# Second SiLU matmul of a three-part kernel: weight sums stationary instead of moving, groups of 1,024 tokens, weight sums streamed

## Chip, cores and metric

One core of a Trainium2 chip runs the whole program. The metric is the time of one execution on the device in microseconds (us); less is better. The number to forecast is the median time of the changed kernel.

## What is computed

Attention with pooled keys gives `x` (4,608 tokens, 512 wide), then two feed-forward blocks follow. The change lies in the second block's last matmul.

```python
x = attn_out.transpose(0, 2, 1, 3).reshape(B * S, H * D)   # 4608 x 512, pooled attention
h = x @ w_in; e = exp(h - max(h)); solu = h * e / sum(e)     # first block, 1024 wide
x = layernorm(solu) * g_ln @ w_out                           # 4608 x 512
h = x @ w2_in                                                # second block, 2048 wide
g = h / (1 + exp(-h))                                        # SiLU
out = g @ w2_out                                             # 4608 x 512, float32
```

## The kernel before

All matmuls are in 32-bit form with each operand split into a high part and a low part (`hi` by a copy on ACT, `lo` by a subtraction on DVE), so that one product of two blocks is three matmuls: high by high, high by low, low by high.

Three parts follow each other. The first, to about 600 us, is attention and the first block. The second multiplies by `w2_in` and applies SiLU: 12 passes (`n`) of four windows (`i`), each window seven products (`product`, L750; tile `m`). It leaves `g`, transposed (features on partitions), in DRAM tiles `gd`, six tiles of 768 tokens. The third part, "the last stage" in what follows, multiplies `g` by `w2_out` (L967, tile `op`). This is the part that changes.

Both SiLU matmuls use Winograd's form of Strassen's scheme: of a 2 x 2 block product seven products are made in place of eight, of sums of blocks. In the last stage the seven sums of `w2_out` are made ahead, during passes 3 to 10 (`w2o_block`, L860), split and written to DRAM as `wod`. The seven sums of `g` are made on the spot.

The products are named after the operand made of `g`: A11, A12 and A22 are raw blocks, S1A, S2A, S3A and S4A sums. The last stage walks over 9 groups of 512 tokens (`c`), 4 sets of contracted features (`s`) and 7 products (`j`). In every one of the 252 steps (`n`, 12 matmuls each) the tokens are the stationary operand (128 x 128) and the weight sum the moving one, 256 columns. All 14.7 MB of weight sums are loaded once and stay in SBUF. `load_g` (L899) fetches the raw blocks of a set, `sums_g` (L919) makes two sums on POOL (tile `s`), `prepare` (L927) makes two more on DVE in place (tile `gr`) and splits the operand into a ring of nine tiles `gt2` (`NRING`), nine steps ahead of the matmul. `combine` (L975) adds a finished product from PSUM to the others on ACT, DVE and POOL and writes `out`. Every engine runs its list in order. The engines' lists in the second and last part are in the order in which the code is written, and every DMA of the last stage stands on SP's list (14 weight loads in pass 11 stand on ACT's).

The second part takes its slots from a table: `plan(n, [(at, f), ...])` puts `f` into slot `at` of 28 in pass `n`, between the products.

Of the kernel before, what the change touches and what calls it, by code (L numbers as in the profile page):

```python
# [40 lines left out]
GO = 512  # L41
NGO = NT // GO
# [7 lines left out]
NSET = FC2 // 4  # L50
NRING = 9
UNITS = ((0, 1, 2), (3,), (4, 5), (6, 7))
# [36 lines left out]
def pooled_attention__solu__silu_kernel(  # L89
# [83 lines left out]
    wod = [dram.tile([P, 7, len(u), 2, 256], F32, tag=f"wod{u[0]}", name="wod") for u in UNITS]  # L173
# [678 lines left out]
    wo, graw, ring = {}, {}, {}  # L852
# [41 lines left out]
    def load_part(u, j, w, eng, first=0, last=None):  # L894
        eng.dma_start(w[:, first:last].bitcast(F32), wod[u][:, j, first:last])
        for i, f in enumerate(UNITS[u]):
            wo[f, j] = w[:, i]

    def load_g(q):  # L899
        c, s = divmod(q, NSET)  # L900
        if q % 3 == 1:
            raw = [pools["wx"].tile([P, 2, GO], F32, tag=f"a{h}", name="gr") for h in range(2)]
        else:
            raw = pools["gr" if q % 3 else "x2r"].tile(
                [P, 2, 2, GO], F32, tag="gr" if q % 3 else "x2r", name="gr")
# [11 lines left out]
    sums = {}

    def sums_g(q, temps):  # L919
        raw = graw[q]  # L920
        a11, a21, a22 = raw[0][:, :, :256], raw[0][:, :, 256:], raw[1][:, :, 256:]
        s1, s2 = (temps(k).rearrange("p (f d) -> p f d", d=256) for k in (1, 2))
        nc.gpsimd.tensor_tensor(s1, a21, a22, op=ALU.add)  # L923
        sub(nc.gpsimd, s2, s1, a11)
        sums[q] = s1, s2

    def prepare(n):  # L927

        q, j = divmod(n, 7)
        raw = graw[q]  # L930
        a11, a21, a12, a22 = (raw[i][:, :, 256 * k : 256 * k + 256] for i in range(2) for k in range(2))
        s1, s2 = sums[q]
        if j == S3A:
            sub(nc.vector, a21, a11, a21)
        src = (a11, s2, s1, a21, a12, a12, a22)[j]
        r = n % NRING
        if r < 7:
            t = pools["wq0"].tile(
                [P, 2, 512], F32R, tag=f"w{(L11, L12, S2, S1, S3, L22, S4)[r]}", name="gt2"
            )  # L940
        else:
            t = pools["wr"].tile([P, 2, 512], F32R, tag=f"w2r{r - 7}", name="gt2")
        ring[n] = t.rearrange("p w (f t) -> p w f t", f=2)
        nc.scalar.activation(ring[n][:, 0], src, AF.Copy)  # L944

        def rest():
            sub(nc.vector, ring[n][:, 1], src, ring[n][:, 0].bitcast(F32))
            if j == A12:
                sub(nc.vector, a12, a12, s2)

        return rest

    o_t = {}

    def product2(n):
        q, j = divmod(n, 7)
        c, s = divmod(q, NSET)
        if s == 0:
            o_t[c, j] = bank("op")
        op = o_t[c, j]  # L960
        t = ring.pop(n)
        for i in range(2):
            w = wo[2 * s + i, j]
            for h in range(2):
                ts = slice(h * P, (h + 1) * P)
                for m, (l, r) in enumerate(((0, 0), (0, 1), (1, 0))):
                    nc.tensor.matmul(  # L967
                        op[:, 256 * h : 256 * h + 256], t[:, l, i, ts], w[:, r],
                        start=(s == i == h == m == 0),
                        stop=(s == NSET - 1 and i == h == 1 and m == 2),  # L970
                    )

    m_t = {}

    def combine(c, j):  # L975
        b = o_t.pop((c, j)).rearrange("p (h d) -> p h d", h=2)

        def temp(name):
            m_t[name] = pools["m2"].tile([P, 512], F32, tag=name, name=name).rearrange(
                "p (h d) -> p h d", h=2)  # L980
            return m_t[name]

        def add(eng, dst, x, y):
            eng.tensor_tensor(dst, x, y, op=ALU.add)

        if j == 0:
            m_t["o"] = pools["ob"].tile([P, 2, 2, DM], F32, tag="ob", name="ob")
            nc.scalar.activation(temp("m1"), b, AF.Copy)
            return
        c11, c12, c21, c22 = (  # L990
            m_t["o"][:, h, :, 256 * d : 256 * d + 256] for h in range(2) for d in range(2)
        )
        r0 = c * GO
        rows = [out[r0 + 256 * h : r0 + 256 * h + 256].rearrange("(t p) d -> p t d", p=P) for h in range(2)]
        if j == 1:
            add(nc.vector, temp("u2"), b, m_t["m1"])
        elif j == 2:
            nc.scalar.activation(temp("m5"), b, AF.Copy)
            add(nc.gpsimd, c12, m_t["u2"], m_t["m5"])
        elif j == 3:  # L1000
            add(nc.vector, temp("u3"), b, m_t["u2"])
            add(nc.gpsimd, c22, m_t["u3"], m_t["m5"])
        elif j == 4:
            add(nc.vector, c11, b, m_t["m1"])
        elif j == 5:
            add(nc.vector, c12, b, c12)
            nc.sync.dma_start(rows[0], m_t["o"][:, 0])
# [160 lines left out]
    banks[:] = [5]  # L1168
# [10 lines left out]
    for n in range(N2):  # L1179
# [28 lines left out]
        if n == N2 - 1:  # L1208
            early = lambda j: pools["te"].tile([P, 3, 2, 256], F32R, tag=f"t{j}", name="w2o")
            work = [(0, lambda: load_g(0)), (8, lambda: load_g(1))]  # L1210
            units = {}

            def two(j):
                units[j] = early(j)
                load_part(0, j, units[j], nc.scalar, 0, 2)

            for j in range(7):
                work += [(3 * j + 1, lambda j=j: two(j)),
                         (21 + j, lambda j=j: load_part(0, j, units[j], nc.scalar, 2))]
            s0 = lambda k: pools["wr"].tile([P, 512], F32, tag=f"w2r{k - 1}", name="s")  # L1220
# [16 lines left out]
    for name in ("gr", "ob", "m2", "w2o"):  # L1237
        open_pool(name, 1, "left")
    load_g(2)
    for j in range(7):  # L1240
        tag = ("raw", "raw", "raw", "w", "w", "w", "sign")[j]
        w = stage.tile([P, 1, 2, 256], F32R, tag=tag, name="w2o", bufs=1 if j == 6 else 3)
        load_part(1, j, w, nc.sync)
    load_g(3)

    def late_part(u):
        for j in range(7):
            w = pools["w2o"].tile([P, 2, 2, 256], F32R, tag=f"w{u}{j}", name="w2o")
            load_part(u, j, w, nc.sync)

    late_part(2)

    def s_tmp(k):
        return pools["m2"].tile([P, 512], F32, tag=f"s{k}", name="s")

    NM = 7 * NSET * NGO
    sums_g(1, s_tmp)
    prepare(7)()
    prepare(8)()
    for n in range(NM):  # L1260
        q, j = divmod(n, 7)
        c, s = divmod(q, NSET)
        product2(n)
        if s == NSET - 1:
            combine(c, j)
        m = n + NRING
        if m < NM:
            if m % 7 == 0 and m // 7 + 2 < NSET * NGO:
                load_g(m // 7 + 2)
                if m == 14:  # L1270
                    late_part(3)
            if m % 7 == 5 and m // 7 + 1 < NSET * NGO:
                sums_g(m // 7 + 1, s_tmp)
            prepare(m)()
# [40 lines left out]
```

## Time and profile before

| | |
|---|---|
| median of 3 runs | 1317.07 us (1317.04 to 1319.51) |
| profiled execution, own time | 1319.98 us |
| its span, first to last instruction | 1318.2 us |
| granted TensorE clock, mean | 0.996 of full speed |
| PE busy, share of the span | 1267.8 us, 96% |
| DVE, ACT, POOL busy | 933.3, 750.2, 507.4 us |
| last stage on PE | 949.17 to 1312.05 us, 3,024 matmuls |

PE is TensorE's matmuls, PEld its weight loads, which lie beside the matmuls. DVE is VectorE, ACT ScalarE, POOL GpSimd, SP the engine that issues DMAs (SPq in a row). A row of the chain that ended last gives when a piece starts, how long it lasts and how many instructions it has. A matmul's own "duration" is its latency, so the pace of a stream of matmuls is read from starts, or from a piece's length divided by its count.

### The profile page before, as it was taken

Reading aid. Unit: us, or ns where it says so; the run is one execution under the profiler, and the core shown is the slowest. Engines: PE = TensorE matmul, PEld = TensorE weight load, DVE = VectorE, ACT = ScalarE, POOL = GpSimd, SP = SyncE. Lnnn points to the kernel's source line nnn. Section 1 sums busy time; section 2 is a strip of 40 time slices with the busy share of each in tenths; the row PEclk is TensorE's granted clock in tenths of the full one; section 3 lists DMA queues with packets and bytes.
Section 4 is the critical chain, followed back from the end, with each engine's and each line's share of the span. In section 5 each row is a group of like instructions: output and inputs, shape, how many; then the busy total and the mean of one; then the engine's idle time right before and its main releaser. Section 6 shows DMA issues by size and latency. Waiting matters only on the chain.

```text
span 1318.2 us, 23218 instructions
## 1 busy us (share of the span) xinstructions
PE 1267.8 (96%) x8192; PEld 1191.3 (90%) x8192; DVE 933.3 (71%) x1426; ACT 750.2 (57%) x1915; POOL 507.4 (38%) x725
## 2 busy tenths in 40 slices
PE   3689999999999999999999999999999999999998
PEld 3578888888888888889999999999999999999998
DVE  6998567776867665665767776666477777778774
ACT  4786566565666565545767777676544444444442
POOL 5666344434443433432324333332134433324331
PEclk9999999999999999999999999999999999999999
DMA  7755345445423411033776697775995443354340
GB/s 223 236 156 178 94 145 151 141 148 154 146 83 105 140 61 73 24 128 118 287 287 253 242 352 271 253 261 205 347 390 171 131 129 121 104 161 129 128 129 33
DMA packets 110101, 226.98 MB, mean 172 GB/s; under 512 B 10784, under 2 KB 44576, under 8 KB 108448
## 3 DMA queue, kind: packets, MB, share of 16 engines
q1 hardware_dynamic: 107968, 219.98, 49.9%
q10 hardware_dynamic: 2016, 5.51, 1.2%
q8 instruction: 65, 1.06, 0.3%
q14 instruction: 52, 0.43, 0.1%
HBM read 141.56 MB, written 83.89 MB: 171 GB/s over the span
## 4 chain that ended last, share of the span: by engine, by line
PE 81%; DVE 5%; ACT 5%; POOL 4%; DMA 2%; issue 2%; SPq 0%; POOLq 0%; ACTq 0%; DVEq 0%
PE op L967 28%; PE m L750 25%; PE hp L448 10%; PE xp L512 8%; PE xp L513 4%; ACT pr L335 2%; PE sp L317 2%; PE tp L497 2%; PE av L422 1%; DMA raw<-vm 1%; PE pm L371 1%; DVE w L148 1%; DMA wr<-w2of 1%; POOL e L483 1%; DVE w L151 1%
## 5 line engine op out<-in xcount | busy, mean ns | idle before, releaser
L967 PE MATMUL op<-w2o,gt 128*128 128x256 f32 x3024 | 363.0, 284 | 0.0
L967 PEld LDWEIGHTS op<-w2o,gt 128*128 128x128 f32 x3024 | 363.0, 192 | 0.0
L750 PE MATMUL m<-t,w2s 128*128 128x384 f32 x2016 | 351.5, 335 | 2.2 <-ACT u L832 1.1
L750 PEld LDWEIGHTS m<-t,w2s 128*128 128x128 f32 x2016 | 349.1, 188 | 4.4 <-ACT u L832 1.8
L512 PE MATMUL xp<-ln,w1oh 128*128 128x512 f32 x576 | 208.9, 404 | 2.0 <-DVE ln L130 1.9
L533 DVE TENSOR_TENSOR gt<-gr,gt 128x512 fp32r<-128x512 f32 x180 | 161.2, 925 | 59.3 <-ACT gt L944 59.0
L944 ACT ACTIVATE gt<-gr 128x512 fp32r<-128x512 f32 x180 | 106.1, 625 | 143.8 <-DVE gr L533 133.0
L513 PE MATMUL xp<-ln,w1ol 128*128 128x256 f32 x576 | 162.4, 282 | 0.0
L335 ACT ACTIVATE pr<-sp,st 128x72 f32<-128x72 f32 x288 | 88.4, 331 | 86.2 <-POOL st L327 86.1
L512 PEld LDWEIGHTS xp<-ln,w1oh 128*128 128x128 f32 x576 | 109.0, 189 | 25.5 <-DVE ln L130 2.5
L448 PE MATMUL hp<-w1ih,xTh 128*128 128x512 f32 x288 | 116.8, 406 | 1.9 <-DVE e L467 1.7
L448 PE MATMUL hp<-w1il,xTh 128*128 128x512 f32 x288 | 113.3, 394 | 1.3 <-POOL w1il L162 1.3
L448 PE MATMUL hp<-w1ih,xTl 128*128 128x512 f32 x288 | 113.6, 394 | 0.9 <-DMA raw<-vm 0.9
L513 PEld LDWEIGHTS xp<-ln,w1ol 128*128 128x128 f32 x576 | 110.1, 191 | 0.1
L923 POOL TENSOR_TENSOR s<-gr 128x512 f32<-128x512 f32 x36 | 58.0, 1611 | 126.9 <-DVE gt L533 72.7
L533 POOL TENSOR_TENSOR tt<-x2r 128x768 f32<-128x768 f32 x22 | 43.4, 1971 | 81.6 <-DMA x2r<-x2d 44.2
L944 ACT ACTIVATE gt<-s 128x512 fp32r<-128x512 f32 x72 | 43.4, 625 | 51.6 <-POOL s L533 31.6
L533 POOL TENSOR_TENSOR s<-s,gr 128x512 f32<-128x512 f32 x36 | 50.0, 1389 | 48.1 <-DVE gr L533 31.0
L448 PEld LDWEIGHTS hp<-w1ih,xTh 128*128 128x128 f32 x288 | 54.6, 190 | 13.7 <-DVE e L467 2.3
L129 ACT ACTIVATE ln<-tp 128x512 fp32r<-128x512 f32 x72 | 39.3, 596 | 48.2 <-PE tp L497 47.8
L448 PEld LDWEIGHTS hp<-w1ih,xTl 128*128 128x128 f32 x288 | 54.5, 189 | 13.2 <-DVE xTl L130 1.5
L448 PEld LDWEIGHTS hp<-w1il,xTh 128*128 128x128 f32 x288 | 54.7, 190 | 11.3 <-POOL w1il L162 1.6
(137 smaller groups left out, 2160.6 us busy)
## 6 DMA issues: line engine op xcount, KB each, us to landing
gr<-gd SPq DMA_DIRECT2D x48, 512.0 KB, 4.8
x2r<-x2d SPq DMA_DIRECT2D x12, 1536.0 KB, 7.5
gd<-ga SPq DMA_DIRECT2D x96, 192.0 KB, 3.1
gd<-gb SPq DMA_DIRECT2D x48, 384.0 KB, 3.2
wod<-wo SPq DMA_DIRECT2D x56, 256.0 KB, 2.5
gr<-gd SPq DMA_DIRECT2D x48, 256.0 KB, 4.2
q<-qT SPq DMA_DIRECT2D x36, 256.0 KB, 3.7
raw<-kT SPq DMA_DIRECT2D x32, 288.0 KB, 3.8
```

The costliest lines, as they stand in the source:

```text
L129: nc.scalar.activation(hi, src, AF.Copy)
L317: nc.tensor.matmul(sp[done : done + n, p // 2, (p % 2) * 2 * SP : (p % 2 + 1) * 2 * SP], q[:, p, done : done + n], kbd[b % 2][:, p, :], st ...
L335: nc.scalar.activation(pr[:, g, h], sv[:, g, h], AF.Exp, scale=SCALE, bias=st[:, 0, g, h : h + 1], accum_out=st[:, 1, g, h : h + 1],)
L448: nc.tensor.matmul(hp[:, f], l, r, start=(n == 1 and m == 0), stop=(n == KC and m == 2))
L497: nc.tensor.transpose(tp[:, k * P : (k + 1) * P], e[:, f, k * P : (k + 1) * P], ident)
L512: nc.tensor.matmul(xp, w1oh[:, k, cs], ln[:, k], start=(k == 0), stop=False)
L513: nc.tensor.matmul(xp[:, :GW], w1ol[:, k, cs], ln[:, k, 0], start=False, stop=(k == FC1 - 1))
L533: eng.tensor_tensor(dst, a, b, op=ALU.subtract)
L750: nc.tensor.matmul(to, wt[:, a, o : o + P], tk[:, b, k], start=(start and k == 0 and m == 0), stop=(k == 1 and m == 2), skip_group_check=n ...
L923: nc.gpsimd.tensor_tensor(s1, a21, a22, op=ALU.add)
L944: nc.scalar.activation(ring[n][:, 0], src, AF.Copy)
L967: nc.tensor.matmul(op[:, 256 * h : 256 * h + 256], t[:, l, i, ts], w[:, r], start=(s == i == h == m == 0), stop=(s == NSET - 1 and i == h ...
```

## The change

The last stage is written anew. What it computes is the same.

- The weight sum is now the stationary operand (two blocks of 128 output features, `blocks`) and the tokens are the moving one, 512 columns (256 in the last group). `out` comes out transposed, 512 x 4,608, and the host turns it round.
- There are 5 groups: four of 2 x 512 tokens and one of 2 x 256. A group is 56 steps: each of the seven products runs over its 8 feature blocks before the next begins, only S2A and S1A take turns (`mixed`). Three of the sums in Winograd's scheme are now made by going on in the same PSUM banks (`CHAIN`).
- `wod` is laid out anew, one DRAM tile for each of the 7 sums. Two sums (S2A, S1A) are loaded once and kept. The other five are streamed from DRAM again for each group, in units of 3, 3 and 2 feature blocks through seven slots (`load_unit`).
- The raw blocks of a whole group (8.4 MB) are held in SBUF, and the next group's blocks are fetched during the present one (`load_raw`, times in `later`).
- The four sums of `g` are made per feature block (`total`), all on DVE, in the first group one of the four on POOL.

```diff
-GO = 512
-NGO = NT // GO
+HD = DM // 2
+GROUPS = ((0, 512), (1024, 512), (2048, 512), (3072, 512), (4096, 256))
-UNITS = ((0, 1, 2), (3,), (4, 5), (6, 7))
+A21 = 7
+NF = FC2 // 2
+STREAM = (A11, A12, A22, S3A, S4A)
+UNITS = ((0, 3), (3, 6), (6, 8))
-    wod = [dram.tile([P, 7, len(u), 2, 256], F32, tag=f"wod{u[0]}", name="wod") for u in UNITS]
+    wod = [dram.tile([P, NF, 2, HD], F32, tag=f"wod{j}", name="wod") for j in range(7)]
...
+    def load_unit(k):
+        c, j, (first, end) = stream[k]
+        w = pools["te"].tile([P, 3, 2, HD], F32R, tag=f"t{SLOTS[k % 7]}", name="w2o")
+        nc.sync.dma_start(w[:, : end - first].bitcast(F32), wod[j][:, first:end])
...
+    mixed = [(S2A, 0)] + [x for f in range(NF - 1) for x in ((S2A, f + 1), (S1A, f))] + [(S1A, NF - 1)]
+    order = [(j, f) for j in (A11, A12, A22) for f in range(NF)] + mixed
+    order += [(j, f) for j in (S3A, S4A) for f in range(NF)]
...
+    def total(c, f, k):
+        if k == 0:
+            eng = nc.vector if c else nc.gpsimd
+            eng.tensor_tensor(sums[c, f], a21, a22, op=ALU.add)
+        elif k == 1:
+            sub(nc.vector, a21, a11, a21)
+        elif k == 2:
+            sub(nc.vector, a11, a22, a21)
         else:
+            sub(nc.vector, a12, a12, a11)
...
-            for h in range(2):
-                for m, (l, r) in enumerate(((0, 0), (0, 1), (1, 0))):
-                    nc.tensor.matmul(op[:, 256 * h : 256 * h + 256], t[:, l, i, ts], w[:, r], ...
+        for d in blocks:
+            for i, (l, r) in enumerate(((0, 0), (0, 1), (1, 0))):
+                nc.tensor.matmul(
+                    acc[c, x][d], w[:, l, P * d : P * d + P], t[:, r],
...
+    for m in range(NM):
+        c, j, f = seq[m]
+        if (c, j) != (last, S4A):
+            product2(m)
+            if f == NF - 1:
+                combine(c, j)
+            if j in STREAM and f + 1 in (e for _, e in UNITS) and free < len(stream):
+                load_unit(free)
+                free += 1
+        n = m + NRING
+        if n < NM:
+            prepare(n)()
+            for f in nxt.pop((seq[n][0], n % 56), ()):
+                f()
+    t = m_t.pop(S2A)
+    for b in range(2):
+        for m in range(NM - NF, NM):
+            product2(m, (b,))
+        nc.vector.tensor_tensor(t[:, b], acc[last, "v"][b], t[:, b], op=ALU.add)
+        write(last, 0, 1, t, b)
```

The orders of the engines' lists up to the last pass of the second part are the same in both kernels. What stands at PE at the start of the last stage, in a row: the tile written, the moving operand, the stationary operand, the shape of the result. Before:

```order
L967 MATMUL op_10474<-w2o_10085,gt2_10226 128x256 x12
L967 MATMUL op_10490<-w2o_10118,gt2_10247 128x256 x12
L967 MATMUL op_10507<-w2o_10148,gt2_10270 128x256 x12
L967 MATMUL op_10524<-w2o_10180,gt2_10292 128x256 x12
L967 MATMUL op_10544<-w2o_10212,gt2_10317 128x256 x12
L967 MATMUL op_10560<-w2o_10245,gt2_10341 128x256 x12
L967 MATMUL op_10596<-w2o_10280,gt2_10364 128x256 x12
L967 MATMUL op_10474<-w2o_10085,gt2_10468 128x256 x6
```

The same place in the changed kernel, with the end of A12 and the middle of A22 in the first group:

```order
L994 MATMUL op_10449<-gt2_10186,w2o_10099 128x512 x3
L994 MATMUL op_10450<-gt2_10186,w2o_10099 128x512 x3
L994 MATMUL op_10449<-gt2_10211,w2o_10099 128x512 x3
L994 MATMUL op_10450<-gt2_10211,w2o_10099 128x512 x3
...
L994 MATMUL op_10555<-gt2_10531,w2o_10198 128x512 x3
L994 MATMUL op_10556<-gt2_10531,w2o_10198 128x512 x3
...
L994 MATMUL op_10662<-gt2_10573,w2o_10209 128x512 x3
L994 MATMUL op_10661<-gt2_10587,w2o_10481 128x512 x3
```

A step was 12 matmuls of 256 columns into one PSUM bank; it is now 2 x 3 matmuls of 512 columns into two banks, and a product stays in its banks for 8 steps in a row.

SP's list in the first third of the last stage, before (raw blocks `gr`, outputs `out`; the weights are all loaded by then):

```order
L913 DMA gr_10705<-gd0_85 128x2x256 x2
L913 DMA gr_10705<-gd1_86 128x2x256 x2
L913 DMA gr_10821<-gd0_85 128x2x256 x2
L913 DMA gr_10821<-gd1_86 128x2x256 x2
L1007 DMA out<-ob_10856 128x2x512
L913 DMA gr_10951<-gd0_85 128x2x256
L913 DMA gr_10952<-gd0_85 128x2x256
```

The changed kernel's list where the first group passes to the second (`w2o` from `wod_111` is A11's sum, from `wod_115` A12's):

```order
L911 DMA gr_10945<-gd2_87 128x2x512
L926 DMA w2o_10962<-wod_111 128x1536
L911 DMA gr_10967<-gd1_86 128x2x512
L911 DMA gr_10987<-gd1_86 128x2x512
L926 DMA w2o_10995<-wod_111 128x1024
L911 DMA gr_11009<-gd1_86 128x2x512
L1012 DMA out<-ob_10930 128x2x512
L1012 DMA out<-ob_10753 128x2x512
L926 DMA w2o_11023<-wod_115 128x1536
L911 DMA gr_11037<-gd1_86 128x2x512
L926 DMA w2o_11056<-wod_115 128x1536
```

Weight loads now stand between raw blocks and outputs throughout the stage, on the one queue.

DVE's list in a steady stretch before (`gt2` is the low part of an operand, `gr` a sum in place, `ob` an addition from PSUM):

```order
L533 TENSOR_TENSOR gt2_10957<-gr_10705,gt2_10957 128x512
L984 TENSOR_TENSOR ob_10856<-op_10596,u3_10911 128x2x256
L533 TENSOR_TENSOR gt2_10974<-s_10915,gt2_10974 128x512
L533 TENSOR_TENSOR gt2_10990<-s_10914,gt2_10990 128x512
L533 TENSOR_TENSOR gr_10705<-gr_10705 128x2x256
L533 TENSOR_TENSOR gt2_11007<-gr_10705,gt2_11007 128x512
L533 TENSOR_TENSOR gt2_11023<-gr_10705,gt2_11023 128x512
L533 TENSOR_TENSOR gr_10705<-gr_10705,s_10915 128x2x256
```

And in the changed kernel, early in the second group:

```order
L536 TENSOR_TENSOR gt2_11045<-gr_10839,gt2_11045 128x512
L954 TENSOR_TENSOR s_11048<-gr_10879,gr_10697 128x512
L536 TENSOR_TENSOR gt2_11058<-gr_10839,gt2_11058 128x512
L536 TENSOR_TENSOR gr_10879<-gr_10839,gr_10879 128x512
L536 TENSOR_TENSOR gt2_11068<-gr_10839,gt2_11068 128x512
L536 TENSOR_TENSOR gr_10839<-gr_10697,gr_10879 128x512
L536 TENSOR_TENSOR gt2_11078<-gr_10839,gt2_11078 128x512
L954 TENSOR_TENSOR s_11081<-gr_10879,gr_10697 128x512
```

DVE has taken over POOL's sums, and in the first part of a group a sum stands behind almost every low part.

## Rows read from the trace of the kernel before

**Rows 1.** The page: span, busy times, granted clock in 40 slices.

```profile
span 1318.2 us, 23218 instructions
PE 1267.8 (96%) x8192; PEld 1191.3 (90%) x8192; DVE 933.3 (71%) x1426; ACT 750.2 (57%) x1915; POOL 507.4 (38%) x725
PEclk9999999999999999999999999999999999999999
```

**Rows 2.** Chain that ended last, in order: start, us, what.

```profile
505.95 5.48 PE hp L448 x24
...
696.05 253.12 PE m L750 x1458
949.17 362.88 PE op L967 x3024
```

**Rows 3.** Timeline of PE: start, duration, engine, line, operands, shape.

```profile
415.85 0.39 PE L448 MATMUL hp<-w1ih,xTl 128*128 128x512 f32 x1
416.08 0.40 PE L448 MATMUL hp<-w1ih,xTh 128*128 128x512 f32 x1
...
417.92 0.40 PE L448 MATMUL hp<-w1ih,xTl 128*128 128x512 f32 x1
418.15 0.28 PE L422 MATMUL av<-pth,vbh 128*128 128x256 f32 x1
```

**Rows 4.** Timeline at the end of the span.

```profile
1299.76 12.28 PE L967 MATMUL op<-w2o,gt 128*128 128x256 f32 x101
...
1312.08 0.69 DVE L984 TENSOR_TENSOR ob<-op,u 128x512 f32<-128x512 f32 x1 [0.68 <-PE op L967]
1312.83 0.37 SPq L1010 DMA_DIRECT2D out<-ob  x1
```

**Rows 5.** DMA issues: queue, count, KB each, median us to landing.

```profile
x2d<-xo SPq DMA_DIRECT2D x72, 128.0 KB, 1.7
out<-ob SPq DMA_DIRECT2D x18, 512.0 KB, 3.9
```

**Rows 6.** DVE groups, 949 to 1318 us: busy us, mean ns, idle before.

```profile
L533 DVE TENSOR_TENSOR gt<-gr,gt 128x512 fp32r<-128x512 f32 x175 | 157.8, 931 | 56.4 <-ACT gt L944 56.1
L533 DVE TENSOR_TENSOR gt<-s,gt 128x512 fp32r<-128x512 f32 x70 | 46.7, 685 | 21.0 <-ACT gt L944 20.9
L533 DVE TENSOR_TENSOR gr<-gr 128x512 f32<-128x512 f32 x35 | 23.8, 681 | 0.0
```

**Rows 7.** Timelines of DVE and of POOL in the last stage.

```profile
1103.60 0.68 DVE L984 TENSOR_TENSOR u<-op,m 128x512 f32<-128x512 f32 x1
1104.20 0.68 DVE L533 TENSOR_TENSOR gr<-gr 128x512 f32<-128x512 f32 x1
...
1109.56 1.75 DVE L533 TENSOR_TENSOR gt<-gr,gt 128x512 fp32r<-128x512 f32 x1 [0.18 <-ACT gt L944]
...
1110.72 1.74 POOL L923 TENSOR_TENSOR s<-gr 128x512 f32<-128x512 f32 x1
```

**Rows 8.** Tile wo: count, duration ns min/median/max, form.

```profile
L533 DVE TENSOR_TENSOR wo<-wr,wo x40: 411/421/2073, 689.7 to 916.3; 128x256 fp32r<-128x256 f32 x40
```

**Rows 9.** ACT groups, 949 to 1318 us.

```profile
L944 ACT ACTIVATE gt<-gr 128x512 fp32r<-128x512 f32 x175 | 102.9, 625 | 141.5 <-DVE gr L533 130.8 <-PE op L967 9.1 <-ACT gt L944 1.1
L988 ACT ACTIVATE m<-op 128x512 f32<-128x512 f32 x9 | 5.4, 598 | 8.8 <-PE op L967 8.7
```

**Rows 10.** Windows: length, PE, PEld, DVE, ACT, POOL busy, clock, DMA share, GB/s.

```profile
680.00:690.00 10.00, 9.81 (x57) 9.49 (x55) 3.69 (x6) 4.44 (x10) 0.69 (x1) 1.00 0.99 372
953.00:990.00 37.00, 37.00 (x311) 37.00 (x310) 29.15 (x34) 16.70 (x28) 11.46 (x9) 1.00 1.04 385
980.00:990.00 10.00, 10.00 (x86) 10.00 (x85) 8.04 (x10) 5.06 (x9) 2.95 (x4) 1.00 1.03 362
1100.00:1200.00 100.00, 100.00 (x836) 100.00 (x835) 77.65 (x102) 41.92 (x73) 36.97 (x25) 1.00 0.42 130
```

**Rows 11.** Timeline of SP's issues at the start of the last stage.

```profile
950.36 0.32 SPq L716 DMA_DIRECT2D gd<-ga  x1
950.77 0.93 SPq L913 DMA_DIRECT2D gr<-gd  x2
```

More of the change, by code (lines that the diff above doesn't have):

```diff
@@ L850, in window @@
             slot(idx, 6)
-    wo, graw, ring = {}, {}, {}
+    wo, raw_g, ring, sums, acc, m_t = {}, {}, {}, {}, {}, {}
     def load_rows(f):
@@ L917, in pooled_attention__solu__silu_kernel @@
[L917 to L937, printed above, removed]
+    HOMES = {
+        A11: (("x2r", "x2r", 0, 6), ("wx", "a0", 6, 8)),
+        A12: (("wx", "a1", 0, 2),) + tuple(("r12", f"r{f}", f, f + 2) for f in (2, 4, 6)),
+        A21: tuple(("r21", f"r{f}", f, f + 2) for f in (0, 2, 4, 6)),
+        A22: tuple(("r22", f"r{f}", f, f + 2) for f in (0, 2, 4, 6)),
+    }
@@ new lines, in pooled_attention__solu__silu_kernel, with load_raw @@
+    CORNER = {A11: (0, 0), A12: (1, 0), A21: (0, 1), A22: (1, 1)}
+    def load_raw(c, j, part):
+        pool, tag, first, end = HOMES[j][part]
+        t = pools[pool].tile([P, end - first, 512], F32, tag=tag, name="gr")
+        h, r = CORNER[j]
+        t0, n = GROUPS[c]
+        done = 0
+        while done < n:
+            g, o = divmod(t0 + r * n + done, G2)
+            m = min(n - done, G2 - o)
+            nc.sync.dma_start(
+                t[:, :, done : done + m], gd[g][:, h * NF + first : h * NF + end, o : o + m]
+            )
+            done += m
+        for f in range(first, end):
+            raw_g[c, j, f] = t[:, f - first, :n]
@@ new lines, in pooled_attention__solu__silu_kernel, with load_kept @@
+    stream = [
+        (c, j, u) for c in range(len(GROUPS)) for j in STREAM for u in UNITS
+    ]
+    SLOTS = (R11, R21, T2, T3, T1, T4, R22)
+    def load_unit(k):
+        c, j, (first, end) = stream[k]
+        w = pools["te"].tile([P, 3, 2, HD], F32R, tag=f"t{SLOTS[k % 7]}", name="w2o")
+        nc.sync.dma_start(w[:, : end - first].bitcast(F32), wod[j][:, first:end])
+        for f in range(first, end):
+            wo[c, j, f] = w[:, f - first]
+    def load_kept(slot, j, f):
+        w = pools["wk2"].tile([P, 2, 2, HD], F32R, tag=f"k{slot}{f}", name="w2o")
+        nc.sync.dma_start(w.bitcast(F32), wod[j][:, f : f + 2])
+        for c in range(len(GROUPS)):
+            for i in range(2):
+                wo.setdefault((c, j, f + i), w[:, i])
@@ new lines, in total, with prepare @@
+    def total(c, f, k):
+        a11, a21, a12, a22 = (raw_g[c, j, f] for j in (A11, A21, A12, A22))
+        if k == 0:
+            sums[c, f] = s_tmp(f)[:, : GROUPS[c][1]]
+            eng = nc.vector if c else nc.gpsimd
[4 more added lines that the diff above has]
+            sub(nc.vector, a11, a22, a21)
+        else:
+            sub(nc.vector, a12, a12, a11)
+    def prepare(m):
+        c, j, f = seq[m]
+        n = GROUPS[c][1]
+        src = sums[c, f] if j == S1A else raw_g[c, {S2A: A11, S3A: A21, S4A: A12}.get(j, j), f]
+        r = m % NRING
+        if r < 2:
+            t = pools["wr"].tile([P, 2, 512], F32R, tag=f"w2r{r}", name="gt2")
+        else:
@@ L938, in prepare @@
             t = pools["wq0"].tile(
[L939 removed]
+                [P, 2, 512], F32R, tag=f"w{(L11, L12, S2, S3, S1, L22, S4)[r - 2]}", name="gt2"
             )
[L941 to L949 removed]
@@ L951, in prepare @@
[L951 to L965, printed above, removed]
-                for m, (l, r) in enumerate(((0, 0), (0, 1), (1, 0))):
[L967 to L971, printed above, removed]
@@ new lines, in prepare, with rest, product2 @@
+        ring[m] = t[:, :, :n]
+        nc.scalar.activation(ring[m][:, 0], src, AF.Copy)
+        def rest():
+            sub(nc.vector, ring[m][:, 1], src, ring[m][:, 0].bitcast(F32))
+        return rest
+    CHAIN = {A11: "u", S2A: "u", S3A: "u", A12: "w", A22: "x", S1A: "v", S4A: "v"}
+    def product2(m, blocks=(0, 1)):
+        c, j, f = seq[m]
+        n, x = GROUPS[c][1], CHAIN[j]
+        first = j in (A11, A12, A22, S1A)
+        if first and f == 0:
+            acc[c, x] = [
+                pools["psb"].tile([P, 512], F32, tag=f"b{b}", name="op")[:, :n] for b in PAIRS[x]
+            ]
+        t, w = ring[m], wo[c, j, f]
+        for d in blocks:
+            for i, (l, r) in enumerate(((0, 0), (0, 1), (1, 0))):
+                nc.tensor.matmul(
+                    acc[c, x][d], w[:, l, P * d : P * d + P], t[:, r],
+                    start=(first and f == i == 0), stop=(f == NF - 1 and i == 2),
+                    skip_group_check=not first,
+                )
@@ new lines, in keep, with write @@
+    def keep(c, j):
+        if j == A22:
+            t = pools["ob"].tile([P, 2, 512], F32, tag="ob", name="ob")
+        else:
+            t = stage.tile([P, 2, 512], F32, tag="raw", name="ob", bufs=3)
+        m_t[j] = t[:, :, : GROUPS[c][1]]
+        return m_t[j]
+    def write(c, r, d, t, b=None):
+        t0, n = GROUPS[c]
+        to = out[HD * d : HD * d + HD, t0 + r * n : t0 + r * n + n].rearrange("(b p) n -> p b n", p=P)
+        if b is None:
+            nc.sync.dma_start(to, t)
+        else:
+            nc.sync.dma_start(to[:, b], t[:, b])
@@ new lines, in pooled_attention__solu__silu_kernel @@
+    SUMS = {A12: ((A11, 0, 0),), S3A: ((S1A, 1, 1), (A22, 1, 0)), S4A: ((S2A, 0, 1),)}
+    def combine(c, j):
+        ps2 = acc[c, CHAIN[j]]
+        if j not in SUMS:
+            t = keep(c, j)
+            for b in range(2):
+                nc.scalar.activation(t[:, b], ps2[b], AF.Copy)
+        for k, r, d in SUMS.get(j, ()):
+            t = m_t.pop(k)
+            for b in range(2):
+                nc.vector.tensor_tensor(t[:, b], ps2[b], t[:, b], op=ALU.add)
+            write(c, r, d, t)
@@ L1208, in pooled_attention__solu__silu_kernel @@
         if n == N2 - 1:
[L1209 to L1220, printed above, removed]
+            work = [(0, lambda: load_raw(0, A11, 0)), (1, lambda: load_raw(0, A11, 1)),
+                    (8, lambda: load_raw(0, A12, 0))]
+            work += [(at, lambda k=k: load_unit(k)) for k, at in enumerate((2, 3, 4, 9, 10, 11, 12))]
             lows = {}
@@ L1236, in pooled_attention__solu__silu_kernel @@
     bt.close()
-    for name in ("gr", "ob", "m2", "w2o"):
+    for name in ("r12", "r21", "r22", "wk2", "sx", "ob"):
         open_pool(name, 1, "left")
[L1239 to L1274, printed above, removed]
+    for i in range(1, 4):
+        load_raw(0, A12, i)
@@ new lines, in pooled_attention__solu__silu_kernel, with later @@
+    nxt = {}
+    def later(c, i, f):
+        nxt.setdefault((c, i), []).append(f)
+    for i in range(4):
+        for j in (A21, A22):
+            if i < 2:
+                load_raw(0, j, i)
+            else:
+                later(0, NRING + 3 * i - 6, lambda j=j, i=i: load_raw(0, j, i))
+        for k, j in enumerate((S2A, S1A)):
+            later(0, NRING + 4 + 3 * i, lambda k=k, j=j, i=i: load_kept(k, j, 2 * i))
+    extras = [
+        (f - i // 3, i) for f in range(NF + 1) for i in range(4) if (f < NF if i < 3 else f)
+    ]
@@ L1277 @@
+    assert not nxt
+    t = m_t.pop(S2A)
+    for b in range(2):
+        for m in range(NM - NF, NM):
+            product2(m, (b,))
+        nc.vector.tensor_tensor(t[:, b], acc[last, "v"][b], t[:, b], op=ALU.add)
+        write(last, 0, 1, t, b)
 def kernel(**inputs):
```

90 lines of the change are left out of this document (29 added, 61 removed).

## Prediction

> **What bounds the kernel now.** I read the page first: PE is busy for 96% of the span and the granted clock stands at nine tenths or more in every slice, the higher of its two levels, 2.4 GHz [rows 1]. So the next view is the chain of work that ended last. Its last two long pieces are PE alone: 1,458 matmuls of the second part in 253.12 us, then all 3,024 of the last stage in 362.88 us without a gap [rows 2]. In the last stage nothing but PE's pace counts. That pace is 362.88 / 3024 = 120.0 ns for 256 columns, while 256 columns at 2.4 GHz are 106.7 ns. So each matmul costs 13.3 ns beside its columns. The same division for the second part, 384 columns, gives 173.6 ns against 160.0, so 13.6 ns. The extra belongs to the matmul, not to its columns.
>
> **PE's new cost.** The columns stay as they were: 4 groups x 56 steps x 6 matmuls = 1,344 of 512 columns, and 56 x 6 = 336 of 256, against 3,024 of 256. Half of the extra goes in the four large groups. For the price of 512 columns the trace has the first block's hidden layer, which also loads new weights for each matmul: 24 in 5.48 us, 228 ns [rows 2], and starts 10 matmuls apart from 415.85 to 418.15 us, 230 ns by rounded starts [rows 3]. 213.3 ns plus 13.3 to 14 gives 226.6 to 227.3. I take 227.5, between the two: 1344 x 227.5 = 305.8 us, 336 x 120.0 = 40.3 us, together 346.1 us, so **16.8 us less**. The ends are 226.6 (18.0 us less) and 230 (13.4 us less).
>
> One rule speaks against this. The Trainium skill (TensorE: Matmul & The Clock Gate, Back-to-back issue gap) gives a warm gap of N / 2.4 plus 2.5 ns. By it the halved matmul count would bring only 1344 x 2.5 = 3.4 us. The rows above show over 13 ns in three widths, so the measurement decides; the rule stays as a rival below.
>
> **The end.** Before, PE ends at 949.17 + 362.88 = 1312.05 us, a DVE addition of 512 columns takes 0.69, and a DMA issued at 1312.83 ends the span at 1318.2 [rows 4]. In the changed kernel the last product is made one block after the other, so the last addition has 256 columns, 0.42 us in the nearest row [rows 8], and the last DMA has 128 KB. A 512 KB output lands after 3.9 us, a 128 KB write after 1.7 [rows 5]. That is 0.27 + 2.2 = **2.4 us less**, with ends of 1 and 3.
>
> **What hides the rest: DVE and ACT.** A step of the large groups lasts 6 x 227.5 = 1.365 us, a group 76.4. DVE has 56 low parts, 32 sums and 8 additions in a group, 96 operations. Where one follows another at once their starts are 0.60 us apart [rows 7]: 57.6 us of 76.4. The dense stretch is the sums': 35 steps, 47.8 us, hold 35 + 32 + 4 = 71 operations, 42.6 us. At 0.685 each [rows 6], as if nothing overlapped, it would be 48.6: 0.8 us late, and the ring's eight steps of lead, 10.9 us, cover that. Without that lead those 0.8 us would be PE's. In the last group a step is 0.72 us, and 71 operations of 0.42 us are 29.8 against 25.2: 4.6 us late at worst, with a lead of 5.8 less one copy and one subtraction (0.8). It just holds. ACT has 56 copies and 8 evacuations of about 0.6 us in a group [rows 9], 39 us of 76.4.
>
> POOL's sums fall away except for eight in the first group. They were what slowed DVE: the low parts made from `gr` took 931 ns in the mean, those made from POOL's result 685 [rows 6], and a DVE operation of 1.75 us ends when POOL's sum begins to run [rows 7]. By (931 - 685) x 175 / 70 sums one POOL sum costs DVE 0.6 us; eight cost 5, inside the 10.9 us of lead.
>
> Where a chain goes on in a bank that ACT has to copy first, PE has other work: S3A follows S2A's end after two S1A steps, 2.7 us, and ACT needs two copies, 1.2 us [rows 9]. In the last group it is 1.44 us against about 0.8.
>
> **What hides the rest: DMA.** This is the new load. Weights: 75 units, seven loaded in pass 11, leave 47.4 MB; kept sums 4.2; raw blocks 35.1; outputs 9.4. Together 96.1 MB in 346 us, 278 GB/s, where the steady last stage had 130 [rows 10]. A full queue moved 385 GB/s over 37 us at this stage's start, with a low of 362 in 10 us, and that with the same kinds of transfers [rows 10]. All stand in order on SP's queue. So the question is the first group, which also loads its own raw blocks and the kept sums. The tightest point is the second group's first A12 weights, step 64, PE at 949.2 + 64 x 1.365 = 1036.5 us. Queued up to there: own raw blocks 5.76 MB, kept sums 4.19, units 7 to 18 8.39, the next group's raw blocks 7.86, three outputs 1.57: 27.8 MB. The queue starts about 951 us, as it did before [rows 11]. At 385 GB/s that is 72 us and 1.7 to land: 1025, 11 us early. At 362 it is 6 us early. It becomes late below 27.8 / 83.5, that is 333 GB/s. A steady group moves 21.0 MB in 76.4 us, 274 GB/s. So DMA costs nothing, and a late SP (its outputs wait for DVE, and the units stand behind them) has seven units of slack, some 19 steps.
>
> Pass 11 gains two ring entries (ACT and DVE have room, PE waits for neither there) and moves weight loads from ACT's list to SP's, ahead of stores whose landing PE doesn't wait for. I cost it at nothing.
>
> **Sum.** 16.8 + 2.4 = 19.2 less, and 0.6 us given back for short waits at the 35 chain ends (an estimate between 0 and 4). Against the profiled execution's own 1319.98 us that is 1301.4; its time lies 2.9 us above the median of the runs, so the median should be 1317.07 - 18.6 = **1298.5 us**.
>
> **Rivals.**
>
> DMA is late (this one can end slower). Weight loads read far more from DRAM, and each 768 KB unit stands behind raw blocks. For it: 334 GB/s are needed in the first group and 362 were the lowest full slice. Against it: no full slice shows less, not even the one with 8 KB strides in DRAM (`w2if`) at 372 [rows 10]. Price: at 320 GB/s step 64 is 3.6 us late (1302); at 300, 9.4 us (1308); at 277 it is 17 us and the gain is gone; below that the steady groups starve too (at 260 GB/s one takes 80.7 us, 4.3 more), and the kernel is slower. The Trainium skill (DMA: Bandwidth & Descriptors, Latency and other measured facts) reports 207 GB/s and less for copies between HBM tensors whose rows stand a large power of two apart, from 512 KiB; the new `wod` has 16 KB, a smaller power of two, and 42, 14 and 28 KB before. By that figure the stage would take 464 us, but no run here shows it for strides this small. Chance 0.13: 0.06 still faster, 0.02 no change, 0.05 slower.
>
> DVE becomes the bound. It decides from 76.4 / 96 = 0.80 us for an operation. At the 931 ns of [rows 6] a group would be 89.4 us, 13 us more, 58 in all: slower. That needs the price to stay without POOL's sums, against which the 685 and 681 of the same rows stand. Chance 0.04; half-way, in the first or last group alone, 3 to 6 us, it counts with the next.
>
> Short waits. Chain ends, the copies of PSUM, the last group's thin lead: 2 to 6 us, 1301 to 1305. Chance 0.13.
>
> The extra isn't halved. If it were 2.5 ns by matmul, the gain would be 3.4 + 2.4: 1311. Three widths speak against it. Chance 0.03.
>
> **Chances and range.** The forecast without more than 1.5 us of waits has 0.67. Faster by over 0.2% (about what a measurement of this kernel can tell from no change, 2.6 us): 0.67 + 0.06 + 0.13 + 0.03 = 0.89; no change 0.02; slower 0.05 + 0.04 = 0.09. The range goes down to 1295.5 (226.6 ns, the larger gain at the end, half a microsecond of scatter) and up to 1308 (DMA at 300 GB/s, all the short waits).
>
> **What would show it.** Right: matmuls of 512 columns 227 to 228 ns apart for the whole of a group, PE without a gap from its first to its last matmul of the stage, about 346 us; DVE near 57 us of 76 in a group; DMA 270 to 390 GB/s; about 4 us from PE's end to the span's. Wrong: PE idle before L994 with a weight load as releaser near 1030 to 1050 us (DMA), or with DVE's low part as releaser (DVE), or a pace away from 227.5 ns.

## The result and the profile after

The changed kernel takes 1298.28 us (median of 4 runs, 1297.32 to 1299.95); the kernel before, with one more run on the same chip, 1318.29 us. The ratio is 0.9849, with a 95% interval from 0.9831 to 0.9867: 1.5% faster. The forecast was 1298.5 us.

The page of the changed kernel, whose profiled execution took 1297.32 us by its own time (beside [rows 1]):

```profile
span 1295.5 us, 20671 instructions
PE 1246.7 (96%) x6848; PEld 1117.8 (86%) x6848; DVE 935.9 (72%) x1529; ACT 774.9 (60%) x1965; POOL 389.4 (30%) x643
PEclk9799999999999999999999999999999999999999
```

PE's share is the same 96% of a shorter span. The clock is at the higher level except for a slice in the first 100 us.

The chain that ended last, its last two pieces (start, us, what; beside [rows 2]):

```profile
693.79 253.07 PE m L753 x1458
946.86 345.11 PE op L994 x1680
```

The second part is as it was, 253 us for the same 1,458 matmuls. The last stage is one piece again, without a gap: 345.11 us after 362.88, **17.8 us less**.

The groups of the last stage (busy us, mean ns of one, idle before):

```profile
L994 PE MATMUL op<-gt,w2o 128*128 128x512 f32 x1344 | 304.9, 389 | 0.0
L536 DVE TENSOR_TENSOR gt<-gr,gt 128x512 fp32r<-128x512 f32 x186 | 130.8, 710 | 49.7 <-ACT gt L974 45.3 <-PE op L994 1.3
L536 DVE TENSOR_TENSOR gr<-gr 128x512 f32<-128x512 f32 x96 | 69.7, 729 | 0.2
L994 PE MATMUL op<-gt,w2o 128*128 128x256 f32 x336 | 40.5, 283 | 0.0
L954 POOL TENSOR_TENSOR s<-gr 128x512 f32<-128x512 f32 x8 | 13.3, 1681 | 50.9 <-DMA gr<-gd 50.9
```

304.9 / 1344 = 226.9 ns for 512 columns, that is 213.3 + 13.6; 40.5 / 336 = 120.5 for 256. PE's idle time is 0.0 in both. The low parts on DVE went from 931 ns to 710 [rows 6].

The windows of the five groups (length, PE, PEld, DVE, ACT, POOL busy, clock, DMA share, GB/s; beside [rows 10]):

```profile
946.86:1023.00 76.14, 76.14 (x337) 62.83 (x336) 64.66 (x91) 36.76 (x64) 13.27 (x8) 1.00 1.02 384
1023.00:1100.00 77.00, 77.00 (x341) 63.78 (x340) 62.17 (x99) 40.40 (x65) 0.00 (x0) 1.00 0.83 280
1100.00:1176.00 76.00, 76.00 (x337) 62.91 (x336) 61.17 (x96) 39.61 (x64) 0.00 (x0) 1.00 0.82 278
1176.00:1252.00 76.00, 76.00 (x339) 63.02 (x338) 58.33 (x98) 37.89 (x65) 0.00 (x0) 1.00 0.69 225
1252.00:1292.00 40.00, 39.95 (x333) 39.75 (x332) 30.24 (x84) 22.03 (x56) 0.00 (x0) 1.00 0.53 200
```

The reader is to see two columns beside PE's. The DMA queue is full for the whole of the first group, 384 GB/s at a share of 1.02, and has room from the second on. DVE works 58 to 65 of 76 us. PE doesn't lose a microsecond to either.

The end of the span, by the timeline (beside [rows 4]):

```profile
1289.57 3.22 SPq L1014 DMA_DIRECT2D out<-ob  x2
1291.99 0.42 DVE L1298 TENSOR_TENSOR ob<-op,ob 128x256 f32<-128x256 f32 x1 [2.45 <-PE op L994]
```

PE ends at 946.86 + 345.11 = 1291.97, the span at 1295.5: 3.5 us, where it was 6.2.

So of the 22.7 us between the two profiled executions 17.8 lie in the last stage, 2.6 at the end, and 2.3 ahead of the last stage, which began at 946.86 instead of 949.17. That last piece can't be put to the change: in the experiments below, with the same list of work up to there, the stage began anywhere from 946.60 to 951.16. Between the medians, 20.0 us, it nearly vanishes.

### The profile page after: what moved, and what is told of

Read it like the earlier page. It is cut to its first block, busy times and chain, and to the rows that moved or that the text cites. A ratio compares the mean times of both kernels' runs of the same rounds, so it can differ in the third digit from the quotient of the medians.

```text
span 1295.5 us, 20671 instructions
## 1 busy us (share of the span) xinstructions
PE 1246.7 (96%) x6848; PEld 1117.8 (86%) x6848; DVE 935.9 (72%) x1529; ACT 774.9 (60%) x1965; POOL 389.4 (30%) x643
## 4 chain that ended last, share of the span: by engine, by line
PE 79%; DVE 6%; POOL 5%; ACT 5%; DMA 3%; issue 2%; SPq 0%; POOLq 0%; ACTq 0%; DVEq 0%
PE op L994 27%; PE m L753 26%; PE hp L451 10%; PE xp L515 7%; PE xp L516 4%; ACT pr L338 2%; PE sp L320 2%; PE tp L500 2%; PE av L425 1%; POOL e L486 1%; DMA raw<-vm 1%; DVE w L151 1%; PE pm L374 1%; DVE w L154 1%; DMA gd<-ga 1%
## 5 line engine op out<-in xcount | busy, mean ns | idle before, releaser
L994 PE MATMUL op<-gt,w2o 128*128 128x512 f32 (+1 forms) x1680 | 345.3, 368 | 0.0
L994 PEld LDWEIGHTS op<-gt,w2o 128*128 128x128 f32 x1680 | 292.6, 189 | 52.6 <-DVE gt L536 0.2
L974 ACT ACTIVATE gt<-gr 128x512 fp32r<-128x512 f32 (+1 forms) x240 | 139.9, 588 | 142.6 <-PE op L994 60.2
L536 DVE TENSOR_TENSOR gt<-gr,gt 128x512 fp32r<-128x512 f32 (+1 forms) x240 | 155.0, 652 | 60.5 <-ACT gt L974 55.8
L536 DVE TENSOR_TENSOR gr<-gr 128x512 f32<-128x512 f32 (+1 forms) x120 | 79.8, 667 | 0.2
L451 PEld LDWEIGHTS hp<-w1ih,xTh 128*128 128x128 f32 x288 | 54.4, 189 | 13.3 <-DVE e L470 2.3
L462 DVE TENSOR_REDUCE ls<-hp 128x1 f32<-128x1024 f32 x36 | 43.6, 1211 | 27.2 <-PE hp L451 27.0
L338 ACT ACTIVATION_READ_ACCUMULATOR pr<-sp,st 128x1 f32 x288 | 62.6, 217 | 0.0
```

The lines of the kernel that those rows point to most:

```text
L338: nc.scalar.activation(pr[:, g, h], sv[:, g, h], AF.Exp, scale=SCALE, bias=st[:, 0, g, h : h + 1], accum_out=st[:, 1, g, h : h + 1],)
L451: nc.tensor.matmul(hp[:, f], l, r, start=(n == 1 and m == 0), stop=(n == KC and m == 2))
L462: nc.vector.tensor_reduce(nm, hp.rearrange("p a n -> p (a n)"), axis=AX, op=ALU.max, negate=True)
L974: nc.scalar.activation(ring[m][:, 0], src, AF.Copy)
L994: nc.tensor.matmul(acc[c, x][d], w[:, l, P * d : P * d + P], t[:, r], start=(first and f == i == 0), stop=(f == NF - 1 and i == 2), skip_g ...
```

## The experiments

All edits are to the changed kernel. It was not run again beside them; on their chips the kernel before took 1318.85 to 1319.86 us, against 1318.29 here, so a difference from the changed kernel's 1298.28 is good to about a microsecond. "Theory" is the prediction's: the gain is the halved count of matmuls at an unchanged extra of each, plus the shorter end, and DMA, DVE and POOL cost nothing.

**Halves.** The same kernel with 256 columns for each matmul. Only the count changes; operands, order, DMA, DVE stay.

```diff
             for i, (l, r) in enumerate(((0, 0), (0, 1), (1, 0))):
-                nc.tensor.matmul(acc[c, x][d], w[...], t[:, r], ...)
+                for k in range(0, n, 256):
+                    nc.tensor.matmul(acc[c, x][d][:, k : k + 256], w[...], t[:, r, k : k + 256], ...)
```

> The changed kernel with each matmul of 512 columns made as two of 256 on the same stationary operand: 3,024 matmuls again, everything else as changed. If each matmul costs 13.3 ns beside its columns, the last stage takes 3024 x 120.0 = 362.9 us, 17.8 more than the changed kernel's 345.1, and the time is about 1316. If the gain came from somewhere else (POOL's sums gone, the kept blocks, the new order), the time stays near 1298.

1317.18 us; the ratio to the kernel before is 0.9989 (0.998 to 0.9999). The chain:

```profile
950.16 362.88 PE op L995 x3024
```

362.88 us for 3,024 matmuls, to the hundredth what the kernel before has in [rows 2], though which operand is stationary, the weights' route, the groups and the sums are all different. So the 17.8 us are the count of matmuls and nothing else in the rewrite. Each matmul has a weight load of its own in both (the pages count as many PEld as PE, 8,192 here and 6,848 in the changed kernel), so the count is that of matmuls with their weight loads; which of the two the 13.3 ns belong to isn't shown.

**Quarters, and thirds.** The same with pieces of 128 columns (the line with a minus), then with 192 + 192 + 128 (the line with a plus).

```diff
-                for k in range(0, n, 128):
+                for k, z in ((0, 192), (192, 192), (384, 128)) if n == 512 else ((0, 128), (128, 128)):
```

> The same with pieces of 128 columns: 6,048 matmuls. If the extra is fixed, one takes 53.3 + 13.6 = 66.9 ns, the stage 404.6 us, the time about 1358. If loading the weights has a pace of its own that 256 columns just hide, the pace stays near 110 to 120 ns (the transposes of 128 columns take 0.87 us for 8) and the time goes to 1620 or more.

1628.96 us, ratio 1.2351 (1.2333 to 1.2369). The second expectation came true, the first didn't.

> The 512 columns as pieces of 192, 192 and 128, the 256 of the last group as 128 and 128: 4,704 matmuls. Pieces of 128 took 111.7 ns each, 45 more than 53.3 + 13.6. If that is a floor for each matmul with its own weights (its columns hide behind it), pieces of 192 (80.0 + 13.6 = 93.6) sit on it too: 4704 x 111.7 = 525 us for the stage, and the time is about 1478. If narrow matmuls are slower per column (two cycles for each below 256 columns), a piece of 192 takes about 165 ns: 1344 x (165 + 165 + 112) + 672 x 112 = 669 us, time about 1622.

One run: 1479.55 us. The chains of the two, quarters first:

```profile
947.50 675.32 PE op L995 x6048
```

```profile
948.95 525.24 PE op L995 x4704
```

675.32 / 6048 = 111.7 ns and 525.24 / 4704 = 111.7 ns. Pieces of 192 and of 128 columns cost the same. In this stage it is a floor for each matmul with weights of its own, 111.7 ns, which 256 columns (120.0) just hide. The Trainium skill (TensorE: Matmul & The Clock Gate, LDWEIGHTS) gives a weight load of P columns P / 1.2 ns, 106.7 for 128; the floor agrees with it within 5 ns, and that the floor is the weight load is the likely reading, not shown apart from this.

**Twice the load on the DMA queue, first attempt.** The first unit of each sum is loaded twice into its slot, then every unit.

```diff
         nc.sync.dma_start(w[:, : end - first].bitcast(F32), wod[j][:, first:end])
+        if k >= 7 and first == 0:        # the second kernel: if k >= 7
+            nc.sync.dma_start(w[:, : end - first].bitcast(F32), wod[j][:, first:end])
```

> The first of the three streamed units of each sum is loaded twice (23 more loads of 768 KB, 18 MB). By the count of bytes up to step 64 the queue then needs 30.9 MB / 83.5 us = 370 GB/s, still under the 385 that a full queue showed: no change, within 2 us of 1298. If transfers of 6 KB rows are slower than those the trace of before showed (under 350 GB/s), PE waits at the second group's first weights: 5 us or more.

> Every streamed unit is loaded twice (47 MB more). Up to step 64 that is 36.2 MB, 433 GB/s needed; at 385 GB/s it comes 10 us late, and each of the next groups needs 31.5 MB / 385 = 81.7 us against 76.4 of PE, 5 us late each: about 20 to 25 us more than the changed kernel, 1318 to 1323. If DMA has far more room than I think (over 430 GB/s), under 5 us more. If the doubled load starves it in another way (SP's issues), more than 40.

1324.13 us (ratio 1.0039, 1.0025 to 1.0054) and 1519.48 us (1.1519, 1.1502 to 1.1536), far over what bytes ask for. In the second the granted clock was also lower, 0.937 in the mean where the changed kernel has 0.994. SP's timeline in the first of the two shows why (L926 is the load, L928 its repetition):

```profile
1032.09 0.34 SPq L926 DMA_DIRECT2D w2o<-wod  x1
1044.27 0.34 SPq L928 DMA_DIRECT2D w2o<-wod  x1
...
1046.83 0.63 SPq L926 DMA_DIRECT2D w2o<-wod  x1
1058.10 0.32 SPq L928 DMA_DIRECT2D w2o<-wod  x1
```

The repetition writes the same slot, so it waits until the first load has landed, 11 to 12 us later on a full queue, and the whole list behind it waits too. Over the stage these waits come to 196 us of SP's time:

```profile
SPq L928 <- DMA w2o<-wod: 196.4, 25, 10.6
```

(in total, how many, the longest). The experiment measured a wait on SP's list, not bandwidth. It was made again without the wait.

**The extra load aside.** The same bytes are copied to DRAM tiles of their own, which nothing waits for; first for 22 of the 68 units, then for all.

```diff
+        if k >= 7 and first == 0:        # the second kernel: if k >= 7
+            x = dram.tile([P, end - first, 2, HD], F32, tag=f"x{k}", name="aside")
+            nc.sync.dma_start(x, wod[j][:, first:end])
```

> The extra load of the first units without a wait on SP's list: for 22 of the 68 units that are loaded in the last stage, a copy of the same 768 KB to a DRAM tile of its own, which nothing waits for (17.3 MB more). Up to step 64 that needs 30.2 MB / 83.5 us = 361 GB/s, a steady group 326, and the first group of the changed kernel moved 384. If bytes decide, the time stays within 2 us of the changed kernel, and the 26 us of the run with two loads into one slot were SP's waits. If it is as slow as that run, the queue itself is full before 384 GB/s.

1297.59 us, ratio 0.9837 (0.9819 to 0.9856): no change, with 17.3 MB more on the queue. The windows of the first two groups:

```profile
946.86:1023.00 76.14, 76.14 (x339) 63.10 (x338) 63.88 (x90) 36.78 (x66) 12.99 (x8) 1.00 1.01 379
1023.00:1100.00 77.00, 77.00 (x341) 63.77 (x340) 62.03 (x98) 40.10 (x65) 0.00 (x0) 1.00 0.98 361
```

The queue is now full for two groups on end, and PE still has no gap.

> The same for all 68 units (47.4 MB more). Up to step 64 that needs 35.4 MB / 83.5 us = 424 GB/s; at 384 it is late by 9 us, and each of the next three groups needs 31.5 MB / 384 = 82 us against 76.4: together 20 to 25 us more than the changed kernel, about 1320. If the copies to DRAM cost the queues more than their bytes, 40 us or more. If under 5, bytes are not what limits the queue.

1319.43 us, ratio 1.0004 (0.9991 to 1.0017), 21 us more than the changed kernel. Three windows of 50 us:

```profile
950.00:1000.00 50.00, 49.88 (x220) 41.00 (x219) 43.84 (x59) 21.91 (x40) 13.11 (x8) 1.00 1.03 391
1000.00:1050.00 50.00, 44.20 (x186) 35.51 (x185) 33.10 (x54) 21.11 (x39) 0.00 (x0) 0.97 1.03 405
1050.00:1100.00 50.00, 50.00 (x222) 41.30 (x221) 38.33 (x63) 26.44 (x43) 0.00 (x0) 1.00 1.03 404
```

The queue is full throughout and gives 391 to 405 GB/s in these windows; PE loses its first microseconds between 1000 and 1050 us. The timeline has the three waits:

```profile
1029.17 4.34 PE L997 MATMUL op<-gt,w2o 128*128 128x512 f32 x18 [0.44 <-DMA w2o<-wod]
1034.97 3.00 PE L997 MATMUL op<-gt,w2o 128*128 128x512 f32 x12 [1.45 <-DMA w2o<-wod]
1041.88 4.35 PE L997 MATMUL op<-gt,w2o 128*128 128x512 f32 x11 [3.92 <-DMA w2o<-wod]
```

Counted by matmuls they stand before steps 59, 62 and 64, and the longest is at the prediction's tightest point. Over the stage PE waited 14.6 us for weight loads. Not all of the 21 us are such waits: from 1040 to 1050 us, behind the longest one, the granted clock was 0.83, so some matmuls ran at the lower of its two levels. The count of bytes up to that point tells the two kernels apart, 361 GB/s asked for and 424.

**POOL's sums back.** POOL makes the first of the four sums in every group.

```diff
-            eng = nc.vector if c else nc.gpsimd
-            eng.tensor_tensor(sums[c, f], a21, a22, op=ALU.add)
+            nc.gpsimd.tensor_tensor(sums[c, f], a21, a22, op=ALU.add)
```

> The changed kernel with the first of the four sums made on POOL in every group, not only in the first: 32 sums move from DVE to POOL. If DVE has the room that the prediction counts, the time stays within 2 us of the changed kernel, while DVE's operations get longer by about 0.6 us for each POOL sum. If taking POOL's work away was part of the gain, it rises by 3 us or more.

1298.2 us, ratio 0.9843 (0.982 to 0.9865): no change. DVE's low parts:

```profile
L536 DVE TENSOR_TENSOR gt<-gr,gt 128x512 fp32r<-128x512 f32 x183 | 147.9, 825 | 40.1 <-ACT gt L973 37.6 <-DMA w2o<-wod 0.7
L953 POOL TENSOR_TENSOR s<-gr 128x512 f32<-128x512 f32 x32 | 52.9, 1686 | 201.0 <-DMA gr<-gd 201.0
```

24 more POOL sums of 512 columns raise DVE's low parts by (825 - 710) x 183 = 21 us, 0.9 us for each sum, and remove 24 x 0.6 us of DVE's own. It comes out near even (DVE's busy time over the span is 938.3 us after 935.9), and PE does not see it.

**More work on DVE.** Every second low part is made twice.

```diff
-            prepare(n)()
+            low = prepare(n)
+            low()
+            if n % 2:
+                low()
```

> Every second low part is made twice (the same numbers again), so DVE has 124 operations in a group where it had 96. At 0.60 us from start to start that is 74.4 us of 76.4: no change, or up to 5 us. At 0.69 us, the duration of one, it is 85.6 us, 9 us more than PE in each large group: 35 to 45 us slower than the changed kernel. From which of the two it is nearer follows how near DVE is to being the bound.

1313.65 us, ratio 0.9959 (0.9945 to 0.9972): 15.4 us more than the changed kernel, between the two. PE's matmuls of the last stage in four windows of 20 us (length, PE, PEld, clock, DMA share, GB/s):

```profile
980.00:1000.00 20.00, 17.27 (x70) 12.19 (x68) 1.00 0.94 372
...
1020.00:1040.00 20.00, 20.00 (x90) 16.57 (x89) 1.00 0.89 345
...
1060.00:1080.00 20.00, 19.29 (x79) 14.11 (x78) 1.00 0.68 250
...
1120.00:1140.00 20.00, 20.00 (x90) 16.57 (x89) 1.00 0.53 198
```

A full window has 90 matmuls. PE's loss lies in one place of each group, the stretch in which the sums are made, and it is largest in the first group, where POOL makes sums beside it and DVE operations last up to 1.78 us; outside it PE runs at its pace. That does not make the dense stretch the bound. The first three groups with all engines, and a piece of DVE's timeline:

```profile
948.00:1031.00 83.00, 79.22 (x337) 61.91 (x336) 77.58 (x111) 36.67 (x64) 13.76 (x8) 1.00 0.93 338
1031.00:1110.00 79.00, 78.29 (x338) 62.70 (x337) 78.00 (x126) 38.91 (x64) 0.00 (x0) 1.00 0.76 269
1110.00:1188.00 78.00, 77.64 (x336) 62.41 (x335) 76.99 (x125) 38.90 (x64) 0.00 (x0) 1.00 0.77 272
```

```profile
1060.26 0.69 DVE L954 TENSOR_TENSOR s<-gr 128x512 f32<-128x512 f32 x1
1060.86 1.41 DVE L536 TENSOR_TENSOR gt<-gr,gt 128x512 fp32r<-128x512 f32 x2
1062.19 1.28 DVE L1027 TENSOR_TENSOR ob<-op,ob 128x512 f32<-128x512 f32 x2
1063.39 0.68 DVE L536 TENSOR_TENSOR gt<-gr,gt 128x512 fp32r<-128x512 f32 x1
```

In the second and third group DVE is busy 78.00 of 79 and 76.99 of 78 us: it has become the bound of the whole group, wherever in it PE waits. A single operation costs 0.60 us from start to start, as predicted, and a low part with its repetition 1.33. So a group asks for 68 x 0.60 + 28 x 1.33 = 78.0 us, and that is what the 336 matmuls of the third group took. The sum over a group decides here.

**A plain end.** The last product is made like the others.

```diff
-        if (c, j) != (last, S4A):
-            product2(m)
+        product2(m)
...
-    for b in range(2):
-        for m in range(NM - NF, NM):
-            product2(m, (b,))
```

> The last product made like all others, both blocks in every step, and added and written at once (two additions of 256 columns, one DMA of 256 KB) in place of one block after the other. The prediction gave 2.4 us to the end, and the trace shows 3.5 us from PE's last matmul to the end of the span, 6.2 before. If the halving at the very end is part of that, the distance grows by 0.33 us for the second addition and about 0.9 for the larger DMA (192 KB took 2.9 us to land, 128 KB 1.7): 4.5 to 5.0 us. If the smaller last group alone did it, it stays at 3.5.

One run, 1299.57 us; the time alone can't tell such a difference, the timeline can. PE's last matmuls and the last two additions:

```profile
1287.75 6.40 PE L994 MATMUL op<-gt,w2o 128*128 128x256 f32 x52
1293.83 0.78 DVE L1027 TENSOR_TENSOR ob<-op,ob 128x256 f32<-128x256 f32 x2 [3.92 <-PE op L994]
```

The same for PE in the changed kernel:

```profile
1285.79 6.16 PE L994 MATMUL op<-gt,w2o 128*128 128x256 f32 x50
```

Here PE ends at 1294.15 and the span at 1297.8, there at 1291.95 and 1295.5: 3.65 and 3.55 us behind PE, the second of the two cases expected. (The chain's piece on PE ends three matmuls earlier in the plain end, where the first of the two additions could start.) The last DMA landed 2.1 us after its issue with 256 KB, 1.7 with 128 KB; but the kernels of the other experiments that end like the changed one have from 3.1 to 3.6 us behind PE, so such a difference is not to be told from that. Practically all of the 2.6 us come from the last group's halved width, which the plain end has too.

## Why the prediction was right

**PE's new cost.** Right. The extra does belong to the matmul (with its weight load): 13.3 ns at 256 columns, 13.6 at 384, 13.6 at 512. I had taken 227.5 ns, above the 226.6 to 227.3 that 13.3 to 14 had given; the run has 226.9, inside them; hence 17.8 us instead of 16.8. Halves bring the whole of it back. The rival of an extra that isn't halved is out. The 2.5 ns that it took from the Trainium skill (TensorE: Matmul & The Clock Gate, Back-to-back issue gap) are there the gap of an isolated matmul, and not what these matmuls show.

The step would have failed below 256 columns. There the cost is 111.7 ns whatever the columns, so "columns plus 13.5 ns" was seen only from 256 up, and 256 was only 8 ns above the floor.

**The end.** 2.6 us against 2.4 (its terms add up to 2.5). The narrower last addition, 0.42 us after 0.69, and the smaller last DMA, landed after 1.7 us where it was 4.4, are as forecast. But the prediction put them to the order of the last product, one block after the other, and that was wrong: the plain end lacks this order and is within 0.1 us of it. It is the last group's 256 tokens that halve the addition and bring most of the smaller DMA.

**DVE and ACT.** Right that they cost nothing. The price from start to start held; DVE's busy time was 58 to 65 us of a group where 57 was named. Doubling every second low part shows how much room there was: less than 28 operations in a group of 96. With them DVE's work over a group, 78.0 us, set the time, as the prediction's count over a group (it decides from 0.80 us for an operation) would have it. The lead of the ring was said to cover what is late in the dense stretch; no run took the lead away. POOL's price on DVE was set at 0.6 us and measured as 0.9, without effect on the sum. One reading of [rows 7] goes too far: the DVE operation of 1.75 us ended 0.6 us after the start that the row gives for POOL's sum, so the row does not show that POOL's sum began to run only then.

**DMA.** Right in what decided: 384 GB/s in the full queue against 385 assumed, 280 in the second group against 274, 281 over the stage against 278. Only the fourth and the last group lie below the 270 to 390 that were named as a sign, at 225 and 200. The weights of the tightest point (step 64) were issued at 1015.54 us and landed 7.5 us later, and PE needed them at 946.86 + 64 x 1.36 = 1034: the forecast had 11 us to spare, and so has the trace. The forecast had only 1.7 us to land, but the issue later, at 1023. (At 362 GB/s its sum gives 7 us to spare, where it says 6.) The rival's condition was tested from both sides: with 361 GB/s asked for nothing changes, with 424 the kernel loses 21 us, which is all of the gain. Rows 16 KB apart in DRAM cost nothing that shows: with all units copied twice the queue gave up to 405 GB/s in the windows shown. The low bandwidth that the prediction cited from the Trainium skill (DMA: Bandwidth & Descriptors, Latency and other measured facts) for large strides plays no part here.

**Short waits.** The 0.6 us given back were not there; PE's idle time in the stage is 0.0. So the forecast of 18.6 less was 1.8 us under the 20.4 that stage and end gave. That the median came out within 0.2 us of 1298.5 is partly luck: the medians differ by 20.0, and the one of before moved up from 1317.07 to 1318.29 with the fourth run.

## What to carry to other kernels

- Before rewriting for wider matmuls, divide a long piece of the chain by its count in each width that the trace has, and subtract the columns at the granted clock. If the same remainder appears in three widths, the gain of a wider moving operand is the number of matmuls saved times it, and it can be taken at its word only where PE is the sole bound of that stage.
- When operands are streamed again and again to make that possible, count the bytes queued up to the first point at which a load is needed, not the mean of the stage: here the mean asked for 278 GB/s, the first group for 333, and 424 would have eaten the whole gain.
- A transfer that waits for an earlier transfer on the same list costs its landing time for everything behind it. Two loads into one slot did more harm than twice the bytes.

## What was not expected

In the last stage a matmul with weights of its own took 111.7 ns, with 128 columns as with 192. The count theory had 66.9 and 93.6 for them. (The first block's transposes of 128 columns, 8 in 0.87 us, take 109 each, so the floor is not the same to the nanosecond everywhere.) The kernel's narrow matmuls of 256 columns had been sitting 8 ns above this floor.
